# Masking the blocks of an attention state: four scaled ScalarE copies in the place of one VectorE product

## The chip, the cores and the metric

The kernel runs on one core of a Trainium2 chip. The time is the device time of one execution in microseconds. TensorE does the matrix products, VectorE (DVE), ScalarE (ACT) and GpSimd (POOL) the elementwise work, and SyncE (SP) issues the transfers. Each engine works through its own queue in the order in which the program was written; semaphores tie the queues together.

## The reference

Three parts follow one another. The first is a chunked linear attention with decay over 4 batches, 8 heads, 768 positions, head width 32 and state width 16:

```
for c in chunks:
    cum = cumsum(log(clip(a)))                       # per head, within the chunk
    M = (C B^T) * exp(cum_i - cum_j) * causal
    y = M x + (C state) * exp(cum_i)
    state = exp(cum_last) * state + sum_j B_j x_j exp(cum_last - cum_j)
```

The heads are then put side by side (256 features, 3072 tokens). The second part is `h = max(x w1, x w2, x w3)` with 768 hidden features and `h w_out`. The third is `h = x w_in` with 2048 hidden features, a rational function of h (cubic polynomial over quadratic), and a product with a second `w_out`. The weights come as 64-bit floating-point numbers, the result is float32.

## The kernel before, in words

The attention works in 6 chunks (NG) of 128 positions (CH). In each chunk there are 8 units (NU): a batch and a half of the heads. A head occupies a part of the 128 partitions, four heads interleaved: partition p belongs to head p mod 4 of its half. For each unit TensorE makes the decay's exponents in PSUM (`d_mm`, lines 482 to 504; ScalarE takes the exponential, line 504), the products of C and B (`s_mm`, line 477), VectorE multiplies the two (`m_op`, line 509), and TensorE makes the output of the chunk (`y_intra`, line 520). The influence of earlier chunks is added from the state (`y_inter`, line 531).

After each chunk but the last, `state(g)` (lines 549 to 580) renews the state. Sixteen products of B with x go into one PSUM buffer of 128 x 512 (line 555), four column blocks of 128, one for each batch. They hold all pairs of four heads; only the pairs of a head with itself are wanted. So the columns are in four groups of 32, one for each head, and on partition p only group p mod 4 may stay. The 0/1 table `own` (128 x 128, loaded with the coefficients into `co_raw`, line 332) says which. The function `mask` (lines 565 to 568) multiplies with it. For the first chunk the masked product is the state itself, in SBUF. For the other four it is masked in place in PSUM, and four VectorE instructions (`upd`, lines 570 to 575) add it to the decayed state before. The PSUM buffer comes from the ring `pd` of two, which the decay exponents of `d_mm` and a product for `e0` (line 455) use too: a decay product two places later waits until the updates have read the buffer.

The weights are converted on the way in, 28 pieces of 256 rows x 256 columns (`plan_conv`, lines 213 to 263): a transfer into one of three raw buffers, two ScalarE steps (lines 246 and 249), three VectorE steps (lines 247, 250 and 253; the last frees the raw buffer), two GpSimd additions (line 258), a ScalarE copy into the high part (line 196) and two GpSimd subtractions for the low part (line 262). 20 pieces belong to the phase of the attention and may run beside it or after it; the last 8 are the second `w_out`.

The order of all this is not written by hand. `Plan` (lines 51 to 153) takes each operation with its engine, an estimated cost, what it reads and writes, and for the matrix products a due time. It works out the latest time of each operation from its followers, then runs a list schedule with the estimated costs: the engine that is free first takes, of the operations that are ready by then, the one with the earliest latest time. The order that results is what each engine's queue gets. The operations of the two later parts (phase 1) are let in when all of the attention (phase 0) is placed. All transfers go through SP's queue, in the planned order, each waiting for its buffer.

The two later parts run column block after column block of 512 tokens, with every float32 product as three products of high and low parts (`mm3`, lines 646 to 652).

Of the kernel before, what the change touches and what calls it, by code (L numbers as in the profile page):

```python
# [13 lines left out]
AF = mybir.ActivationFunctionType  # L14
ALU = mybir.AluOpType
# [3 lines left out]
NB, NH, SEQ, HD, NS = 4, 8, 768, 32, 16  # L19
CH = 128  # L20
# [30 lines left out]
class Plan:  # L51
# [16 lines left out]
    def op(self, engine, cost, fn, reads=(), writes=(), at=None, behind=()):  # L68
        i = len(self.ops)
        deps, after = set(), {w for t in behind for w in t.writers}  # L70
        for t in reads:
            assert (t.writers or t.given) and not t.closed
            deps.update(t.writers)
            t.readers.append(i)
        for t in writes:
            assert not t.closed
            if t.first is None:
                t.first = i
                if t.before and not t.before.given:
                    after.add(t.before.first)  # L80
                if t.prev:
                    t.prev.closed = True
                    deps.update(t.prev.writers + t.prev.readers)
            deps.update(t.writers + t.readers)
            t.writers.append(i)
        deps.discard(i)
        after.discard(i)
        self.ops.append((engine, cost, fn, [t for t in writes if t.first == i], deps, after, at,
                         self.phase))
# [67 lines left out]
def decay_attention_max_moe_rational_moe(  # L157
# [19 lines left out]
    act, dve, pool, pe = nc.scalar, nc.vector, nc.gpsimd, nc.tensor  # L177
# [93 lines left out]
    op = plan.op  # L271
    pools = {"mp1": mp1}

    def new(pl, tag, size, shape=(128, T), dtype=F32):
        return plan.tile(tag, size, lambda: pools[pl].tile(list(shape), dtype, tag=tag, name=tag))
# [56 lines left out]
    own = co_raw[:, 6:]  # L332
# [76 lines left out]
    for p in range(3):  # L409
        src = pcv if p == 0 else (lambda p=p: cr(p - 1))  # L410
        op("act", 0.3, lambda p=p, src=src: copy(act, cs[:, p], src()), [pc if p == 0 else cr_t], [cs_t])
        if p < 2:
            op("dve", 0.34, lambda p=p, src=src: dve.tensor_tensor(out=cr(p), in0=src(), in1=cs[:, p],
                                                                   op=ALU.subtract),
# [9 lines left out]
    def load_cum(g):  # L424
# [12 lines left out]
        out=sel.rearrange("r (q n f) -> r q n f", q=2, f=4),  # L437
        in_=ld[1][0:24, :, 0].rearrange("r (q f) -> r q f", q=2)[:, :, None, :].to_broadcast([24, 2, NS, 4])),
# [5 lines left out]
    def book(key, cost):  # L444
        when[key] = clock[0]
        clock[0] += cost
# [102 lines left out]
    def state(g):  # L549
        t = new("pd", "d", 2)  # L550

        def mm():
            for b in range(NB):
                for q in range(2):
                    pe.matmul(t.t[64 * q:64 * q + 64, 128 * b:128 * b + 128],
                              bg[g].t[:, 2 * b + q].rearrange("j n f -> j (n f)"),
                              xg[g].t[:, b, 128 * q:128 * q + 128],
                              start=(b == 0), stop=True, skip_group_check=True,
                              tile_position=(0, 64 * q))
        book(("st", g), 0.6)  # L560
        op("pe", 0.6, mm, [bg[g], xg[g]], [t], when["st", g])
        st[g + 1] = o = new("s2", "st", 2)


        def mask(out):
            dve.tensor_tensor(out=out.rearrange("p (b x) -> p b x", b=NB),
                              in0=t.t.rearrange("p (b x) -> p b x", b=NB),
                              in1=own[:, None, :].to_broadcast([128, NB, CH]), op=ALU.mult)

        def upd():  # L570
            for b in range(NB):
                c = slice(128 * b, 128 * b + 128)
                dve.scalar_tensor_tensor(
                    out=o.t[:, c], in0=st[g].t[:, c], scalar=e0[g].t[:, 128 * b + 127:128 * b + 128],
                    in1=t.t[:, c], op0=ALU.mult, op1=ALU.add)
        if g == 0:
            op("dve", 0.68, lambda: mask(o.t), [t, own_t], [o])
        else:
            op("dve", 0.68, lambda: mask(t.t), [own_t], [t])
            op("dve", 1.2, upd, [t, e0[g], st[g]], [o])  # L580

    plan.phase = None
# [15 lines left out]
    for s in range(NS_ALL + LEAD + 3):  # L598
        if s < NS_ALL:
            d_mm(s)  # L600
            if s % NU == NU - 1 and s // NU + 2 < NG:
                load_cum(s // NU + 2)
        u = s - LEAD
        if 0 <= u < NS_ALL:
            g, k = divmod(u, NU)
            if u % 2 == 0:
                s_mm(u)
            m_op(u)
            if k == NU - 1 and g + 2 < NG:
                load_s(g + 2)  # L610
            if k == 4 and g + 1 < NG:
                prep(g + 1)
        u = s - LEAD - 1
        if 0 <= u < NS_ALL:
            g, k = divmod(u, NU)
            y_intra(u)
            if k == 2 and g < NG - 1:
                state(g)
            if k == 3 and g:
                y_inter(g)  # L620
            if k >= NU - 2:
                y_out(g, k - NU + 2)
            if k == NU - 1 and g + 2 < NG:
                load_v(g + 2)
# [343 lines left out]
```

## Time and profile before

| | us |
|---|---|
| median of 3 runs | 578.93 (577.61 to 580.32) |
| profiled execution | 579.21 |
| its span | 577.3 |
| TensorE busy | 556.8 (96%) |
| VectorE busy | 511.9 (89%) |
| ScalarE busy | 435.3 (75%) |
| GpSimd busy | 440.6 (76%) |

The span runs from the first to the last instruction of the profiled execution. Busy times are sums over the span; an engine can be idle for long in one stage and full in another. The mean granted clock of TensorE is 0.997 of full speed.

### The profile page before, as it was taken

The page shows a single profiled execution, that of the slowest core. Times are in us where ns is not written, and L with a number is a line of the kernel's source. Part 1 is how long each engine was busy: PE and PEld are TensorE (multiplying, and loading weights), DVE is VectorE, ACT ScalarE, POOL GpSimd, SP SyncE. Part 2 cuts the span into 40 slices and gives each one's busy share as a digit, 9 for nine tenths or more (in the row PEclk, how much of TensorE's full clock was granted, in tenths as well). Part 3 has the DMA queues.
Part 4 walks back from the last instruction along what each step waited for, and adds up shares of the span by engine and source line. Part 5 has one row for each costly group of instructions (what it writes and reads, how often), then busy time and mean ns, then how long its engine had stood idle before and what let it go on. Part 6 is the DMA issues. An engine that isn't in the chain of part 4 may idle for free.

```text
span 577.3 us, 8164 instructions
## 1 busy us (share of the span) xinstructions
PE 556.8 (96%) x2747; PEld 411.2 (71%) x2758; DVE 511.9 (89%) x777; ACT 435.3 (75%) x756; POOL 440.6 (76%) x410
## 2 busy tenths in 40 slices
PE   8989989989999999999999999999999999999997
PEld 3333433768787788888888888888888888886563
DVE  7888979777999999998889988898898889988996
ACT  4677768556888878878788787778777877778883
POOL 1756767887989967778677877687777997869883
PEclk9999999999999999999999999999999999999999
DMA  6877864533000000101000010000000010000000
GB/s 216 243 270 238 237 233 148 182 110 109 1 1 2 18 20 0 37 1 38 0 1 37 1 33 6 0 20 18 1 1 1 0 37 0 1 1 36 2 0 36
DMA packets 19047, 33.71 MB, mean 58 GB/s; under 512 B 3526, under 2 KB 4030, under 8 KB 19006
## 3 DMA queue, kind: packets, MB, share of 16 engines
q1 hardware_dynamic: 19003, 33.20, 17.9%
q8 instruction: 21, 0.34, 0.2%
q14 instruction: 23, 0.16, 0.1%
HBM read 27.27 MB, written 5.91 MB: 57 GB/s over the span
## 4 chain that ended last, share of the span: by engine, by line
PE 53%; DVE 17%; POOL 17%; issue 4%; ACT 4%; DMA 3%; SPq 2%; POOLq 0%; ACTq 0%; DVEq 0%
PE pg L650 7%; PE pg L652 7%; PE pg L651 6%; PE ph L650 5%; PE ph L652 5%; PE ph L651 5%; PE po L652 4%; PE po L650 4%; PE po L651 4%; POOL glo L853 2%; PE s L477 2%; DMA wraw<-in_w_dram 2%; POOL v L819 2%; POOL hlo L295 2%; DVE pr L845 2%
## 5 line engine op out<-in xcount | busy, mean ns | idle before, releaser
L853 POOL TENSOR_TENSOR glo<-w,ghi 128x512 fp32r<-128x512 f32 x80 | 105.5, 1319 | 16.2 <-ACT ghi L196 16.1
L650 PE MATMUL pg<-xhi,w_hi 128*128 128x512 f32 x202 | 79.1, 392 | 2.8 <-DVE xa L732 2.2
L652 PE MATMUL pg<-xhi,w_lo 128*128 128x512 f32 x202 | 78.8, 390 | 0.0
L651 PE MATMUL pg<-xlo,w_hi 128*128 128x512 f32 x202 | 78.7, 390 | 0.0
L840 ACT ACTIVATE pr<-v,qc 128x512 f32<-128x512 f32 x83 | 57.4, 693 | 22.2 <-DVE v L826 11.3
L295 POOL TENSOR_TENSOR hlo<-xa,hhi 128x512 fp32r<-128x512 f32 x36 | 49.5, 1376 | 26.0 <-ACT hhi L196 25.9
L258 POOL TENSOR_TENSOR wa<-wa,we 128x256 uint32<-128x256 uint32 x56 | 44.2, 800 | 32.9 <-DVE wa L253 32.9
L196 ACT ACTIVATE ghi<-w 128x512 fp32r<-128x512 f32 x80 | 50.4, 630 | 23.9 <-PE po L652 14.2
L650 PE MATMUL ph<-yhi,win_hi 128*128 128x512 f32 x160 | 62.7, 392 | 1.7 <-DVE w L838 1.5
L651 PE MATMUL po<-glo,wo_hi 128*128 128x512 f32 x160 | 62.4, 390 | 0.4 <-POOL glo L853 0.4
L652 PE MATMUL ph<-yhi,win_lo 128*128 128x512 f32 x160 | 62.3, 390 | 0.0
L650 PE MATMUL po<-ghi,wo_hi 128*128 128x512 f32 x160 | 62.3, 390 | 0.0
L652 PE MATMUL po<-ghi,wo_lo 128*128 128x512 f32 x160 | 62.3, 390 | 0.0
L651 PE MATMUL ph<-ylo,win_hi 128*128 128x512 f32 x160 | 62.3, 389 | 0.0
L845 DVE SCALAR_TENSOR_TENSOR pr<-w,co,pr 128x512 f32<-128x512 f32 x83 | 61.9, 746 | 0.0
L819 POOL TENSOR_TENSOR v<-t,v 128x512 f32<-128x512 f32 x44 | 58.1, 1320 | 2.8
L842 DVE SCALAR_TENSOR_TENSOR v<-v,pr 128x512 f32<-128x512 f32 x83 | 56.2, 677 | 2.2 <-ACT pr L841 2.2
L847 DVE SCALAR_TENSOR_TENSOR w<-v,pr 128x512 f32<-128x512 f32 x83 | 56.3, 678 | 0.4
L841 ACT ACTIVATE pr<-pr 128x512 f32<-128x512 f32 x86 | 50.5, 587 | 0.9
L732 DVE TENSOR_TENSOR xa<-xa,pg 128x512 f32<-128x512 f32 x67 | 45.5, 679 | 2.3 <-PE pg L652 2.1
L650 PEld LDWEIGHTS pg<-xhi,w_hi 128*128 128x128 f32 x202 | 37.9, 188 | 12.1 <-DVE xa L732 3.1
L837 POOL TENSOR_TENSOR w<-w,t 128x512 f32<-128x512 f32 x20 | 25.9, 1293 | 24.0 <-DVE v L826 22.1
(167 smaller groups left out, 1485.1 us busy)
## 6 DMA issues: line engine op xcount, KB each, us to landing
wraw<-in_wo_dram SPq DMA_DIRECT2D x11, 512.0 KB
wraw<-in_w_dram SPq DMA_DIRECT2D x9, 512.0 KB
wraw<-in_win_dram SPq DMA_DIRECT2D x8, 512.0 KB
xn<-in_xn_dram SPq DMA_DIRECT2D x6, 512.0 KB
out_dram<-ob SPq DMA_DIRECT2D x12, 256.0 KB
xt_d<-xo SPq DMA_DIRECT2D x10, 256.0 KB
xst<-xt_d SPq DMA_DIRECT2D x10, 256.0 KB
bt<-in_bz_dram SPq DMA_DIRECT2D x6, 256.0 KB
```

The costliest lines, as they stand in the source:

```text
L196: act.activation(out=o, in_=i, func=AF.Copy)
L295: lambda: e.tensor_tensor(out=lo.t, in0=src(), in1=hi.t.bitcast(F32), op=ALU.subtract),
L650: pe.matmul(dst, wh, hi, start=first, stop=False)
L651: pe.matmul(dst, wh, lo, start=False, stop=False)
L652: pe.matmul(dst, wl, hi, start=False, stop=last)
L819: pop(1.23, lambda: pool.tensor_tensor(out=f(v), in0=f(t1), in1=f(v), op=ALU.mult), [t1], [v])
L840: aop(0.62, lambda: act.activation(out=f(r), in_=f(v), func=AF.Ln, bias=qc), [v], [r])
L841: aop(0.48, lambda: act.activation(out=f(r), in_=f(r), func=AF.Exp, scale=-1.0), [], [r])
L842: dop(0.61, lambda: dve.scalar_tensor_tensor(out=f(v), in0=f(v), scalar=QC, in1=f(r), op0=ALU.add, op1=ALU.mult), [r], [v])
L845: dop(0.61, lambda: dve.scalar_tensor_tensor(out=f(r), in0=f(w), scalar=c(0), in1=f(r), op0=ALU.add, op1=ALU.mult), [w], [r])
L847: dop(0.61, lambda: dve.scalar_tensor_tensor(out=f(w), in0=f(v), scalar=2.0, in1=f(r), op0=ALU.subtract, op1=ALU.mult), [v, r], [w])
L853: pop(1.23, lambda: pool.tensor_tensor(out=f(lo), in0=f(w), in1=f(hi).bitcast(F32), op=ALU.subtract), [w, hi], [lo])
```

## The change

The mask goes from VectorE to ScalarE. Column group f of every batch block (4 blocks x 32 columns) is copied with a scale that is read per partition: the column 32 f of `own`, which is 1 on the partitions of head f and 0 on the others. Four such copies make the mask. The planner is told that the operation is ScalarE's and costs 1.2 us, where it was VectorE's and 0.68. What is read and written is unchanged, in place for four of the five states.

```
         def mask(out):
-            dve.tensor_tensor(out=out.rearrange("p (b x) -> p b x", b=NB),
-                              in0=t.t.rearrange("p (b x) -> p b x", b=NB),
-                              in1=own[:, None, :].to_broadcast([128, NB, CH]), op=ALU.mult)
+            for f in range(4):
+                act.activation(out=out.rearrange("p (b f d) -> p f b d", b=NB, f=4)[:, f],
+                               in_=t.t.rearrange("p (b f d) -> p f b d", b=NB, f=4)[:, f],
+                               func=AF.Copy, scale=own[:, HD * f:HD * f + 1])
...
         if g == 0:
-            op("dve", 0.68, lambda: mask(o.t), [t, own_t], [o])
+            op("act", 1.2, lambda: mask(o.t), [t, own_t], [o])
         else:
-            op("dve", 0.68, lambda: mask(t.t), [own_t], [t])
+            op("act", 1.2, lambda: mask(t.t), [own_t], [t])
             op("dve", 1.2, upd, [t, e0[g], st[g]], [o])
```

## Rows read from the trace of the kernel before

**Rows 1.** Stretches: us, busy (x instructions) by engine, granted clock, DMA share, GB/s.
```profile
0.00:30.00 30.00, 26.67 (x149) 10.75 (x151) 23.58 (x41) 17.39 (x31) 13.52 (x19) 1.00 0.79 229
30.00:60.00 30.00, 27.31 (x255) 11.82 (x260) 27.45 (x50) 23.20 (x43) 20.08 (x23) 1.00 0.77 256
60.00:100.00 40.00, 34.67 (x341) 14.69 (x345) 35.54 (x61) 30.03 (x54) 28.36 (x37) 1.00 0.65 206
100.00:130.00 30.00, 27.20 (x117) 21.26 (x118) 22.65 (x29) 17.33 (x31) 25.39 (x29) 0.95 0.42 143
130.00:190.00 60.00, 58.32 (x254) 47.22 (x253) 54.45 (x79) 47.44 (x84) 53.90 (x52) 1.00 0.08 27
190.00:500.00 310.00, 310.00 (x1369) 256.75 (x1368) 280.80 (x413) 241.59 (x411) 240.91 (x198) 1.00 0.04 13
```

**Rows 2.** Groups of the mask's line on VectorE: busy us, mean ns, idle before.
```profile
L566 DVE TENSOR_TENSOR d<-d,co_raw 128x512 f32<-128x512 f32 x4 | 2.8, 689 | 0.4 <-PE d L555 0.4
...
L566 DVE TENSOR_TENSOR st<-d,co_raw 128x512 f32<-128x512 f32 x1 | 0.7, 692 | 0.0
```

**Rows 3.** ScalarE groups with each shape apart, whole span.
```profile
L825 ACT ACTIVATE v<-ph,co 128x512 f32<-128x512 f32 x40 | 27.1, 677 | 0.0
...
L816 ACT ACTIVATE v<-ph 128x512 f32<-128x512 f32 x40 | 23.8, 595 | 2.7 <-PE ph L652 2.1
...
L840 ACT ACTIVATE ph<-v,qc 128x256 f32<-128x256 f32 x1 | 0.5, 479 | 0.5 <-POOL v L810 0.5
...
L841 ACT ACTIVATE ph<-ph 128x256 f32<-128x256 f32 x1 | 0.4, 368 | 0.0
...
L440 ACT ACTIVATE co<-co_raw 128x2 f32<-128x2 f32 x1 | 0.2, 193 | 0.0
```

**Rows 4.** Timeline by engine, 48 to 55 us: start, us, instruction, idle before and releaser.
```profile
49.17 1.09 PE L555 MATMUL d<-xn,bn 128*64 128x128 f32 x16
...
52.77 0.39 PE L488 MATMUL d<-trib 128*128 128x512 bf16 x1 [0.83 <-DVE st L573]
...
50.32 0.70 DVE L566 TENSOR_TENSOR d<-d,co_raw 128x512 f32<-128x512 f32 x1 [0.36 <-PE d L555]
50.93 0.75 DVE L250 TENSOR_SCALAR wa<-wa 128x512 uint32<-128x512 uint32 x1
51.60 1.11 DVE L573 SCALAR_TENSOR_TENSOR st<-st,e,d 128x128 f32<-128x128 f32 x4
...
49.80 0.66 ACT L249 ACTIVATE we<-wraw 128x512 uint32<-128x512 uint32 x1
50.37 0.58 ACT L504 ACTIVATE e<-d 128x512 f32<-128x512 f32 x1
51.43 0.68 ACT L246 ACTIVATE wa<-wraw 128x512 f32<-128x512 f32 x1 [0.48 <-POOL w_lo L262]
```

**Rows 5.** Timeline by engine, 79 to 88 us.
```profile
82.27 1.09 PE L555 MATMUL d<-xn,bn 128*64 128x128 f32 x16
...
84.94 0.37 PE L455 MATMUL d<-re,sel 24*128 24x512 bf16 x1 [0.68 <-ACT e L504]
85.69 0.38 PE L488 MATMUL d<-trib 128*128 128x512 bf16 x1 [0.38 <-DVE st L573]
...
83.58 0.69 DVE L566 TENSOR_TENSOR d<-d,co_raw 128x512 f32<-128x512 f32 x1
...
84.52 1.11 DVE L573 SCALAR_TENSOR_TENSOR st<-st,e,d 128x128 f32<-128x128 f32 x4
...
84.29 0.60 ACT L504 ACTIVATE e<-d 128x512 f32<-128x512 f32 x1 [1.05 <-PE d L490]
```

**Rows 6.** Waits of TensorE, 0 to 100 us: total us, times, longest.
```profile
PE d L488 <- DVE st L573: 1.2, 2, 0.8
```

**Rows 7.** Waits of SP's queue, 0 to 100 us.
```profile
SPq L241 <- DVE wa L253: 17.3, 6, 6.3
SPq L283 <- PE y L531: 2.3, 2, 1.3
```

## The prediction

> **What bounds the kernel now.** I read first the busy time by stretch [rows 1], then the group of the line that goes [rows 2], the ScalarE groups that give the price of what comes [rows 3], and the instructions around the single states [rows 4, 5], last the waits [rows 6, 7].
>
> The stretches show three regimes. From 190 to 500 us TensorE is busy 310.0 of 310.0: nothing that happens in the attention stage reaches that part except by moving it as a whole. From 0 to 100 us the attention runs with the conversion of the weights between its instructions: TensorE is busy 26.67 + 27.31 + 34.67 = 88.65 us, VectorE 23.58 + 27.45 + 35.54 = 86.57, ScalarE 17.39 + 23.20 + 30.03 = 70.62. From 100 to 190 the first products run beside the last conversions; TensorE lacks 2.80 us of 30 and 1.68 of 60 there, and its granted clock is 0.95 in the first of the two stretches [rows 1]. So all that an edit of the attention can gain or lose is TensorE's idle time before 190 us, 11.35 + 4.48 = 15.8 us, plus what the lower clock costs; much of the 11.35 is start-up, before any state exists. VectorE has 13.4 us of slack in the first 100 us and ScalarE 29.4. That alone speaks for moving work from VectorE to ScalarE, but a stage with every engine at 70 to 90% and a written order on each is bound by whichever result comes last, now of one engine, now of another. The question is which states' masks lie on such a chain.
>
> **The change part by part.** *Removed:* five VectorE products, four in PSUM of 689 ns and one into SBUF of 692 ns [rows 2], 4 x 0.689 + 0.692 = 3.45 us of VectorE. In the queue each takes a little less than it lasts, since the next starts before its end.
>
> *Added:* twenty ScalarE copies, each 128 partitions x 128 elements in runs of 32, with a per-partition scale. The trace has no such instruction, so I take it from its neighbours [rows 3]. From PSUM without a per-partition operand 512 elements take 595 ns, with one (a scale) 677: 82 ns for the operand. Without one, 256 elements take 368 ns and 2 elements 193: (368 - 193) / 254 = 0.69 ns an element, while 256 to 479 ns with one is 111 ns more. So 128 elements: 193 + 0.69 x 126 + 82 = 362 ns, at most 391 with the 111. Neighbours in the queue overlap: the 0.66 us instruction at 49.80 is followed at 50.37, 0.09 us before its end [rows 4]. Four in a row: 3 x (0.37 - 0.09) + 0.37 = 1.21 us. Bounds: 4 x 0.193 = 0.77 us if the length cost nothing and nothing overlapped, and 4 x 0.479 = 1.92 us if the runs of 32 made each as dear as the 256-element one with its operand. I take 1.21, nearest to the row of the same operand count, so five masks are 6.0 us of ScalarE (3.9 to 9.6). None hides on its own; what hides it is ScalarE's 29.4 us of slack.
>
> The Trainium skill (ScalarE: Activation LUTs, What ACT_TABLE_LOAD costs) gives 186 ns + 0.833 ns an element, about 93 more for a per-partition operand, and 93 of overlap. By it a copy would be an estimated 386 ns and four 1.27 us, and the forecast would not move. The same page (Rules for kernel authors) would keep multiplications on VectorE. In instruction time the trace agrees, 0.69 us against 1.21; what the rule leaves out is how full either engine is, and that it speaks against this change is the second rival below.
>
> *Moved, state by state.* A state's path is: state products on TensorE, mask, four updates on VectorE, then the two-buffer PSUM ring is free for the next decay product and the state for the inter-chunk products. All waits of the decay product on the update sum to 1.2 us in 2 cases, 0.8 the longer [rows 6]. So of five masks only two are felt; the other three have slack, and their longer mask (1.21 - 0.69 = 0.52 us and a hand-over between engines) costs nothing there.
>
> The first felt state [rows 4]: the state products end at 49.17 + 1.09 = 50.26. The product starts at 50.32 and ends at 51.02, but VectorE then does a conversion step until the updates start at 51.60. With ScalarE, which finishes a conversion instruction at 50.46 and has an exponential next, the mask could run from 50.37 to 51.58, and with a hand-over like the 0.06 us between TensorE and VectorE just seen, up to some 0.2, the updates start at 51.64 to 51.78: 0.04 to 0.18 us later. TensorE waited 0.83 us there, so this goes straight into the end. If the exponential at 50.37 goes first, add its 0.58. The other way, the conversion step that stood between can go ahead of the updates at no cost; a gain there is excluded by the mask's end. I take +0.1 (bounds 0 to +0.8).
>
> The second [rows 5]: the state products end at 83.36, the mask ran 83.58 to 84.27, the updates from 84.52, and TensorE waited 0.38 for them at 85.69. ScalarE was idle until 84.29. The mask on it runs 83.42 to 84.63, the updates start at 84.7 to 84.8: +0.2 to +0.3. The exponential of 84.29 moves to 84.54 or later; the product at 84.94 had waited 0.68 for it, so it moves by 0.25 too, alongside, not on top. I take +0.25 (bounds 0 to +1.2, if the mask goes behind that exponential and a conversion).
>
> *The relief of VectorE:* behind each mask the queue moves up by 0.69 us at most. What is late next? The weight transfers stand in SP's queue until the last conversion step on VectorE frees a raw buffer: 17.3 us of such waits in 6 cases before 100 us [rows 7]. Each earlier release brings a transfer, its ScalarE steps and GpSimd's work forward. But ScalarE's own steps of the same conversion go back by the 1.21 us of a mask. At the first felt state a conversion step stood right behind the mask, at 50.93 [rows 4], and such a step could come 0.69 us earlier; as the two effects meet in one conversion I count half of that once, -0.35 (bounds 0 and -3.45, all five masks).
>
> Sum: +0.1 + 0.25 - 0.35 = 0.0 us. The profiled execution took 579.21 us, its span 577.3 and 1.9 around it; that is 0.28 above the median of the runs, 578.93, and inside their spread of 577.61 to 580.32. Forecast: 579.2 us, no change.
>
> **Rivals.** *First, VectorE is the true bound of 30 to 100 us.* For it: it is busy 27.45 of 30 and 35.54 of 40, and holds the raw buffers [rows 1, 7]. Then all 3.45 us come off: 579.2 - 3.45 = 575.8. Against it: TensorE is busy 27.31 of the same 30, so most of what VectorE gives up is met by TensorE's own queue, and what is gained in the conversions counts only as far as it fills the 4.48 us that TensorE lacks between 100 and 190 us.
>
> *Second, slower: ScalarE's queue is held at the mask.* Its place is the head of ScalarE's queue when the four copies wait for the state products. VectorE waited 0.36 us in that position at 50.32 [rows 4]; behind the copies on ScalarE stand exponentials, for which TensorE already waits (0.68 at 84.94 [rows 5]), and the conversion's absolute value, low word and high part, for which VectorE and GpSimd wait. Price: 0.36 + 1.21 = 1.57 us of ScalarE for each state. It decides once ScalarE has less idle time near a state than that. Around the states at 50 and 84 it had 0.48 and 1.05 us [rows 4, 5], so the point is near. With three crowded states of five, 3 x 1.57 = 4.7 us less what VectorE's relief returns, 0.35: 583.6. Nor does it end there: the inter-chunk products are later with the state, and the loads behind them in SP's in-order queue (2.3 us in 2 cases already [rows 7]) and the weights behind those. Against it: 29.4 us of slack over the stage, and the planner knows of the copies, as it is given 1.2 us for them.
>
> *Third, the order is drawn anew.* The planner sees other costs and engines, so all queues of the attention and its conversions may come out differently, not only around the masks. Then the stall of TensorE between 100 and 130 us, 2.80 us and about 0.05 x 30 = 1.5 us by the clock [rows 1], may vanish or double: 574.9 or 583.5. For it: the stage has 48 decay products and 28 conversions that can slide past one another. Against it: their due times are those of before.
>
> *Fourth, the copies cost what the dear bound says,* 1.92 us: (1.92 - 1.21) x 2 felt states = +1.4 us, 580.6; this stays within no change.
>
> **How the numbers follow.** Forecast with the fourth 0.50; VectorE the bound 0.18; ScalarE held 0.23; the new order 0.09, of it 0.05 to the slow side. About 0.5% is what a measurement of this kernel can tell from no change, 2.9 us either way of 578.93. Faster: 0.18 + 0.04 = 0.22. Slower: 0.23 + 0.05 = 0.28. Same: 0.50. The forecast's own range is 576.9 to 581.4: below it the lowest of the runs, 577.61, less twice the 0.35; above it 579.2 with the 0.8 of the first felt state and the 1.4 of the dear copies. To leave out no more than 2 in 10 the range reaches to the first rival on one side and past the second on the other: 575.3 to 584.2.
>
> **What would show it.** Right: in the profile after, twenty copies of about 0.36 us, four in about 1.2; VectorE 3.4 us less and ScalarE about 6 more by the sum of the busy time; the wait of the decay product on the updates still 1 to 2 us in all; TensorE still full from about 190 us. The first rival shows as fewer waits of SP's queue on the conversion step, and a TensorE that is full earlier. The second shows as ScalarE waiting for the state products by name, and more waits of TensorE on exponentials. The third shows as another order of conversions, and another idle time between 100 and 130 us. The prediction is wrong if TensorE's idle time before 190 us changes by over 3 us in either direction.

## The result, and the profile after

Over 22 executions each, the kernel after takes 582.52 us (579.47 to 585.43) and the kernel before 578.92 (576.93 to 582.95): a ratio of 1.0051, interval 1.0036 to 1.0066. That lies inside the stated range and at the 0.5% from which the prediction called a kernel slower: the interval reaches to both sides of it. The most likely case, no change at 579.2 us, was 3.3 us off. An execution over 1.5% longer than the fastest of its kernel (there is one, of the copies told 0.68 us below) is left out of its time and ratio.

The profiled execution after took 582.59 us, its span 580.8. Its stretches, in the columns of [rows 1]:

```profile
0.00:30.00 30.00, 26.50 (x151) 10.88 (x152) 23.57 (x40) 18.41 (x36) 13.21 (x19) 1.00 0.80 238
30.00:60.00 30.00, 26.41 (x228) 11.37 (x227) 24.57 (x45) 22.07 (x44) 16.73 (x21) 0.89 0.69 226
60.00:100.00 40.00, 35.29 (x315) 14.58 (x314) 33.99 (x55) 32.51 (x63) 30.10 (x39) 1.00 0.68 222
100.00:130.00 30.00, 27.49 (x169) 20.44 (x168) 23.30 (x35) 18.93 (x33) 24.94 (x28) 1.00 0.40 142
130.00:190.00 60.00, 57.98 (x249) 46.27 (x250) 53.25 (x76) 47.25 (x83) 52.97 (x52) 1.00 0.08 27
190.00:500.00 310.00, 310.00 (x1369) 256.78 (x1368) 280.72 (x414) 241.68 (x410) 240.12 (x197) 1.00 0.04 13
```

From 190 to 500 us TensorE is as full as before, so all was decided earlier. The change shows between 30 and 60 us: 228 matmuls were done there, 255 before [rows 1], at a granted clock of 0.89. Some matmul records are missing in the trace of before; by the weight loads, the counts of the next column, of which none is missing, it is 227 and 260. The groups of the mask and of the update, with each shape apart:

```profile
L567 ACT ACTIVATE d<-d,co_raw 128x128 f32<-128x128 f32 x16 | 5.4, 340 | 2.0 <-PE d L555 1.5
...
L574 DVE SCALAR_TENSOR_TENSOR st<-st,e,d 128x128 f32<-128x128 f32 x16 | 4.5, 342 | 4.3 <-ACT d L567 4.3
...
L567 ACT ACTIVATE st<-d,co_raw 128x128 f32<-128x128 f32 x4 | 1.1, 368 | 0.4 <-PE d L555 0.4
```

VectorE now waits 4.3 us for the copies. TensorE's waits of 0 to 100 us, the answer to [rows 6]:

```profile
PE d L488 <- ACT e L504: 1.9, 3, 1.2
PE y L520 <- ACT e L504: 1.4, 1, 1.4
...
PE s L477 <- DVE m L509: 0.9, 1, 0.9
PE y L520 <- ACT xo L196: 0.9, 1, 0.9
...
PE d L455 <- DVE st L574: 0.4, 1, 0.4
```

The wait on the updates, 1.2 us before, is down to 0.4: the state's own path is not where TensorE waits. It waits for exponentials, products and output copies that are placed otherwise. Three instructions of the timeline show the low clock and the state whose products begin at 37.85 us. The first, the four records of a pair of C and B products, spans 3.00 us here and 1.13 at 41 us; not all of that is the clock, as the same pair takes 2.06 at a clock of 1.00 in the profile of the experiment below that fills TensorE's idle time:

```profile
31.97 3.00 PE L477 MATMUL s<-cz,bt 64*128 64x512 f32 x4 [0.92 <-DVE m L509]
...
39.65 1.47 ACT L567 ACTIVATE d<-d,co_raw 128x128 f32<-128x128 f32 x4 [1.53 <-PE d L555]
...
41.15 1.12 DVE L574 SCALAR_TENSOR_TENSOR st<-st,e,d 128x128 f32<-128x128 f32 x4 [3.79 <-ACT d L567]
```

Read alone, this profile has a ready story. TensorE's idle time is the same (577.3 - 556.77 = 20.5 us before, 580.8 - 559.79 = 21.0 after), and its busy time is 3.0 us longer, because matmuls from 32 to 39 us ran at the lower of its two clock levels, 1.2 GHz. A part of it falls with the count of the records of line 490, the second matmul of a decay product, first before, then after:

```profile
L490 PE MATMUL d<-lr x29: 376/379/380, 24.1 to 94.8; 128*128 128x512 bf16 x29
```

```profile
L490 PE MATMUL d<-lr x40: 377/379/634, 24.6 to 103.9; 128*128 128x512 bf16 x40
```

Eleven are missing before, and the gaps that they leave (0.05 to 0.15 us each) sum to 1.3 us that are counted as idle. So TensorE is an estimated 1.7 us longer busy and 1.8 us longer idle. The profiles of the copies in the old order, the product in the new order, the copies to SBUF and the idle time filled lack the same kind of record, 11 each, and can be compared with one another. The experiments show that what is left of the story belongs to this one execution.

### The profile page after: what moved, and what is told of

The parts are those of the page before. It is cut to its first block, busy times and chain, and to the rows that moved or that the text cites. A ratio compares the mean times of both kernels' runs of the same rounds, so it can differ in the third digit from the quotient of the medians.

```text
span 580.8 us, 8190 instructions
## 1 busy us (share of the span) xinstructions
PE 559.8 (96%) x2758; PEld 411.9 (71%) x2758; DVE 509.5 (88%) x772; ACT 442.4 (76%) x776; POOL 439.5 (76%) x410
## 4 chain that ended last, share of the span: by engine, by line
PE 50%; POOL 20%; DVE 17%; issue 5%; ACT 5%; DMA 2%; SPq 0%; POOLq 0%; DVEq 0%; ACTq 0%
PE pg L651 6%; PE pg L652 6%; PE pg L653 6%; PE ph L651 4%; PE ph L652 4%; PE ph L653 4%; PE po L651 4%; PE po L652 4%; PE po L653 4%; POOL glo L854 3%; POOL wa L258 3%; POOL hlo L295 2%; POOL v L820 2%; DVE wa L253 2%; POOL wo_lo L262 2%
```

## The experiments

Three theories. A: the new order of all queues costs, whatever makes the mask. B: the copies cost, by their length and by what stands behind them on ScalarE. C: the clock costs. The second set split A: any new order is a draw (A1), a plan with the mask on ScalarE is worse as such (A2), the plan was given too low a cost (A3). Each set of kernels was timed against the kernel before in five rounds on one chip; there were three sets, so compare ratios, not times, between sets.

**The copies in the order of before.** In the kernel after, only what the planner is told goes back:

```
-            op("act", 1.2, lambda: mask(t.t), [own_t], [t])
+            op("dve", 0.68, lambda: mask(t.t), [own_t], [t])
```

and so for the first state. Apart from the mask, all five queues then hold the instructions of before in their order; the two traces agree on that instruction by instruction.

> The four ScalarE copies, but the planner is still told that the mask is VectorE's and costs 0.68 us, so all queues keep the order of before and the copies stand in ScalarE's queue where the program reaches them. If the new order is what costs (theory A), the time is that of before, 579 plus or minus 1 us. If the copies themselves on ScalarE cost (theory B: 1.45 us in place where the product took 0.69, and what stands behind them), it is that of the change, about 582.5.

Measured: 580.08 us, ratio 1.0016 (1.0002 to 1.0029): 0.1 us above the upper end of what theory A expected, 2.4 below theory B.

**The product in the order of the change.** The opposite edit in the kernel before: the VectorE product, told as `"act", 1.2`.

> The VectorE product, but the planner is told that the mask is ScalarE's and costs 1.2 us, so all queues have the order of the change. Theory A (the order): about 582.5 us, with TensorE idle from 28.7 to 32 us and its granted clock low in 30 to 40 us, as after the change. Theory B (the copies): 579 plus or minus 1.

Measured: 582.29 us, ratio 1.0060 (1.0036 to 1.0083). So the order alone gives the whole of the 0.51%, and without it the copies cost 0.16%, 0.9 us. Theory A stands and, of B, those 0.9 us are left. The stretch of 30 to 60 us in the two profiles, first the copies in the old order:

```profile
30.00:60.00 30.00, 27.61 (x255) 11.96 (x259) 26.15 (x48) 25.34 (x50) 20.37 (x23) 1.00 0.78 256
```

and the product in the new order:

```profile
30.00:60.00 30.00, 25.50 (x223) 11.04 (x226) 24.72 (x45) 20.84 (x38) 17.05 (x23) 0.89 0.69 220
```

255 matmuls and 223, as in the kernels before and after, 255 and 228 (by weight loads 259 and 226, 260 and 227); the count follows the order, not the engine of the mask.

The executions of that set also bear on C. Their mean granted clock over the span was 0.9953 for the kernel before (26 executions) and 0.9952 for the product in the new order (10). Among those with 0.997 or more, the medians are 578.6 us (10 executions) and 581.6 (5). The difference of 3.0 us is there at an equal clock. The clock moves both kernels: before from 576.65 us at 1.000 to 582.15 at 0.991, the product in the new order from 579.87 at 1.000 to 583.95 at 0.991.

**TensorE's idle time filled.** In the kernel after:

```
-            for q, t in enumerate(ts):
+            for q, t in [z for z in enumerate(ts) for _ in range(2 if u == 10 else 1)]:
...
-            op("pe", 0.46, lambda: mm(lambda: ld[g % 2][:, k], lambda: rd[g % 2]),
+            op("pe", 0.46, lambda: [mm(lambda: ld[g % 2][:, k], lambda: rd[g % 2]) for _ in range(3 if u == 12 else 1)],
```

> The change, but TensorE repeats two products of which the results stay the same: the sixth pair of C and B products once more (1.06 us) and the thirteenth decay product twice more (0.9 us), just before and in its idle time of 28.7 to 32 us. If the drop of the granted clock after that idle time is what costs (theory C), the clock stays at its upper level from 30 to 40 us and the time falls by about 3 us, to 579.5, though work was added. If the order costs by its waits alone, the time stays at 582.5 or rises by up to 1.

Measured: 581.59 us, ratio 1.0038 (1.0020 to 1.0056). Its stretch:

```profile
30.00:60.00 30.00, 25.58 (x234) 11.24 (x238) 25.93 (x46) 23.64 (x48) 17.78 (x23) 1.00 0.71 228
```

The clock is 1.00 now, and still only 234 matmuls are done, four of them repeats, and the kernel is 0.38% slower than before. Of the 3 us that C promised 0.8 came by the ratios (1.0051 to 1.0038), and the intervals of this kernel and the one after overlap. The mean clock of its nine executions is 0.998, that of the kernel after 0.996. In this profile and in that of the copies in the old order the clock is 1.00 throughout the attention, so TensorE's idle time can be compared: 30 - 25.58 = 4.42 us here from 30 to 60 us, 30 - 27.61 = 2.39 there. The other stretches up to 190 us differ by 0.2 together (14.56 and 14.32). In these two profiles, what the new order costs in idle time lies between 30 and 60 us.

**The copies to SBUF.** In the kernel after, in the order of the change:

```
+    ms = [sp.tile([128, T], F32, name=f"ms{i}") for i in range(2)]
...
-                    in1=t.t[:, c], op0=ALU.mult, op1=ALU.add)
+                    in1=ms[g % 2][:, c], op0=ALU.mult, op1=ALU.add)
...
-            op("act", 1.2, lambda: mask(t.t), [own_t], [t])
+            op("act", 1.2, lambda: mask(ms[g % 2]), [own_t], [t])
```

> The change, but the four later states are copied from PSUM into an SBUF buffer instead of in place; the planner is told the same, so the order is that of the change. If masking in place makes each copy wait for the one before, four copies take 1.14 us as for the first state, not 1.46. Theory B then expects up to 4 x 0.3 = 1.3 us less, 581.2; theory A no difference beyond 0.5 us, 582.5.

Measured: 582.65 us, ratio 1.0060 (1.0038 to 1.0083), no gain. The copies did get shorter in a row: on ScalarE the mask of the third state is

```profile
53.23 1.14 ACT L568 ACTIVATE ms<-d,co_raw 128x128 f32<-128x128 f32 x4
```

against 1.46 in place. In place the program makes each copy wait on ScalarE's own semaphore for the one before it, and they start 0.36 to 0.37 us apart; to SBUF it does not, and they start 0.25 to 0.27 apart. But the updates, which now read two operands from SBUF, took twice as long:

```profile
L575 DVE SCALAR_TENSOR_TENSOR st<-st,e,ms 128x128 f32<-128x128 f32 x16 | 10.0, 686 | 1.0 <-ACT ms L568 1.0
```

**More buffers for the output copies.** In the kernel after, `xo = new("s4", "xo", 2)` for `new("s2", "xo", 2)`: four real buffers, two in the plan.

> The change, with four SBUF buffers in place of two for the copied-out outputs xo; the planner still counts two, so the order is that of the change to the last instruction. In that order the output copy of the second chunk waits 1.0 us on ScalarE for a VectorE subtraction that was placed late, and TensorE 0.9 to 1.3 us behind it at 48 to 50 us. If that wait is a part of what the order costs, the two waits vanish and the time falls by 0.5 to 1.3 us, to 581.2 to 582.0; if TensorE meets the next wait instead (the exponential before the state products, 0.7 us), under 0.3 us.

Measured: 583.72 us, ratio 1.0066 (1.0040 to 1.0092): nothing gained. The 0.9 us wait for the output copy is gone between 38 and 64 us; all of TensorE's waits that this stretch has are

```profile
PE y L520 <- DVE m L509: 1.9, 1, 1.9
PE d L455 <- DVE st L574: 0.6, 1, 0.6
PE d L488 <- ACT e L504: 0.4, 1, 0.4
```

The next wait took its place. The one wait that was tried does not carry the 3 us.

**Other orders.** Nothing but the cost that the planner is told of the mask is changed, in the kernel after (1.5, 0.9, 0.68 for 1.2) and in the kernel before (0.6, 0.8, 1.0 for 0.68).

> The change, but the planner is told 1.5 us for the four copies, near the 1.46 that they take in place; the order is drawn anew by that. Theory A1 (any new order is a draw, the time of a drawn order scatters by some us whoever makes the mask): anywhere from 578 to 585. Theory A2 (a plan with the mask on ScalarE is worse as such): 582 to 584. Theory A3 (the plan was worse since its cost was too low): 579 to 580.

> The change, but the planner is told 0.9 us for the four copies. A1: anywhere from 578 to 585, with no line through 0.9, 1.2 and 1.5. A2: 582 to 584. A3: 583 to 585, worse than with 1.2, since the cost is further off.

> The kernel before, with the VectorE product, but the planner is told 0.60 us for it (what it holds VectorE's queue for) in place of 0.68. Nothing that runs is changed but the order. A1: anywhere from 577 to 584, away from 579.5 by 1 us or more with even chances. A2: 579.5 plus or minus 1.

> The change, but the planner is told that the ScalarE copies cost 0.68 us, what it was told of the product. A1 (each order is a draw): anywhere from 580 to 586. A2 (a plan with the mask on ScalarE is worse as such): 582 to 584, as with 0.9 and 1.2.

> The kernel before, but the planner is told 0.8 us for the product. The order is nearer to that of before than any other drawn here. If a few places decide (A1 with a local cause), within 1 us of 579; if any redrawing costs since the order of before is a lucky one, 581 to 584, as with 0.6.

> The kernel before, but the planner is told 1.0 us for the product; an order further from that of before. A1: anywhere from 579 to 585, and not better for being nearer to what the planner was told of the copies. A2 (only ScalarE's plan is worse): 579 plus or minus 1.

Measured, with the change itself:

| mask by | cost told, us | time, us | ratio to before |
|---|---|---|---|
| VectorE | 0.60 | 582.64 | 1.0069 (1.0043 to 1.0095) |
| VectorE | 0.68 | before | 1 |
| VectorE | 0.80 | 580.89 | 1.0027 (1.0007 to 1.0046) |
| VectorE | 1.00 | 582.65 | 1.0048 (1.0026 to 1.0070) |
| ScalarE | 0.68 | 583.64 | 1.0072 (1.0048 to 1.0097) |
| ScalarE | 0.90 | 583.09 | 1.0074 (1.0047 to 1.0101) |
| ScalarE | 1.20 | 582.52 | 1.0051 (1.0036 to 1.0066) |
| ScalarE | 1.50 | 593.01 | 1.0234 (1.0210 to 1.0258) |

With the product unchanged, a told cost that is 0.08 us lower makes the kernel 0.69% slower, more than the change did: A1 is shown. A3 falls, as 1.5 is nearest to the measured 1.46 and far the worst. A2 as it was expected, with VectorE's plans within 1 us of before, falls too, by 0.60 and 1.00. That ScalarE's plans are worse on the average isn't settled: they are 0.51 to 0.74% and 2.34% slower, those with VectorE 0.27 to 0.69%, and the intervals overlap. The order nearest to that of before, 0.80, came out at 580.89 us, between the two times that were expected of it, and decides nothing. All seven new orders are slower than that of before; why that one is the best of eight stays open.

A new order can cost by the clock too. The executions told 0.60, 0.80 and 1.00 have mean clocks of 0.9923, 0.9946 and 0.9928, those of before in their sets 0.9961 and 0.9957. The two told 1.00 with 0.997 took 578.60 and 579.78 us, while 13 of before with 0.997 have a median of 579.40: for that order no loss is seen at an equal clock. The copies told 0.90 lost 0.74% at 0.9963, as high as before. With 1.5 the stretch of 30 to 60 us is

```profile
30.00:60.00 30.00, 25.21 (x189) 9.68 (x190) 22.73 (x36) 20.21 (x40) 17.43 (x21) 0.77 0.65 217
```

and there the clock matters most: all four executions had a mean of 0.981 to 0.986. In its profile TensorE is busy 565.42 us and its span is 591.1. Of 13.8 us more than before, 8.65 are busy time and 5.2 idle; with the 1.3 us of records that are missing before, an estimated 7.4 and 6.4.

**The product to SBUF.** In the kernel before, in its own order, the four later masks go to SBUF and the updates read them there, with the two edits of the copies to SBUF.

> The kernel before in its own order, but the four later products go from PSUM into an SBUF buffer, from which the updates read, so that the PSUM buffer comes free 1.1 us earlier. TensorE waited 1.2 us for it in 2 cases: if that is worth its length, 578.0 to 578.5, better than both kernels. But with the copies to SBUF the updates took 0.81 us instead of 0.34 at the median; if it is the SBUF operand that does this and not the order, VectorE loses up to 16 x 0.47 = 7.5 us and the time is 580 to 583.

Measured: 579.55 us, ratio 1.0004 (0.9990 to 1.0019), the same. The updates:

```profile
L574 DVE SCALAR_TENSOR_TENSOR st<-st,e,ms 128x128 f32<-128x128 f32 x16 | 6.2, 444 | 0.0
```

at 444 ns instead of the 335 to 342 with the mask in PSUM. The earlier release of the PSUM buffer bought nothing measurable. TensorE's wait on the updates is gone from 0 to 100 us, but the decay product waits 2.1 us for exponentials, where it waited 1.3 before. No version that was tried beats the kernel before.

## Why the prediction was right or wrong

**The range and the sum.** The range held the time, in part by luck: no change was forecast, and the range reached to 584.2 for the second rival, whose cause was not the one. The sum of 0.0 us was worked out instruction by instruction in the order of before, and for that order it was off by the 0.9 us of the copies in the old order. What failed is the step beneath it: the sum carried the old order over to the changed kernel. The instructions around the states at 50 and 84 us [rows 4, 5], on which it rests, have other neighbours after the change.

**The sign of being wrong.** TensorE's idle time before 190 us went from 15.83 to 16.33 us, an estimated 1.8 us more with the missing records, so the sign set at 3 us did not show. It looked at one execution of each kernel, and at idle time alone.

**The copy's price.** Forecast 0.36 us each and 1.21 for four; measured 0.368 and 1.14 for the first state, which goes to SBUF. In place one is 0.340, but four take 1.46, since each waits for the one before. The overlap of 0.09 us in the sum was the term at fault, 1.46 against 1.21, inside the bounds of 0.77 to 1.92. ScalarE got 5.4 + 1.1 = 6.5 us of copies where 6.0 were forecast, and its busy time rose by 442.4 - 435.3 = 7.1; VectorE's fell by 2.4, not 3.4.

**The felt states.** Forecast +0.1 and +0.25 at two states, and the wait on the updates at 1 to 2 us in all. In the profile after, it is 0.4; it is 0.3 with the copies in the old order and 1.3 with the product in the new order. VectorE's queue takes the wait: 4.3 us after, 3.8 of it at one state, while TensorE had other products to do.

**VectorE's relief.** Counted at -0.35. No run shows it by itself. The copies in the old order, with VectorE relieved and ScalarE loaded, were no faster; the first rival, which had 3.45 us come off, is refuted by that.

**The second rival,** ScalarE held at the mask, named the right sign and nearly the time (583.6), but the wrong cause: with the copies and all that stands behind them in the old order, 0.9 us is what was left of 4.7. ScalarE did wait for the state products, 1.5 us once, as that rival said; it cost little. TensorE's waits on the exponentials of line 504 from 0 to 100 us rose from 3.2 us to 4.0, but to 4.6 with the product in the new order: they too go with the order.

**The third rival,** the order drawn anew, is what happened. It had a chance of 0.09 and 0.05 on the slow side. The time it gave, 583.5, was near; its place, TensorE's stall of 100 to 130 us, was not: idle time there is 2.51 us after and 2.80 before [rows 1], and the loss sits between 30 and 60 us. Its argument against, that the due times were those of before, carried no weight: in the attention due times are given to matmuls alone, and all else follows from the told costs. A told cost that changes on an operation between engines should have had most of the chance for a change, with a width of some us, in place of the 0.50 for none; all seven draws here fell on the slow side.

What stays open: why an order with fewer matmuls done from 30 to 60 us isn't caught up, and which of its places decides. One wait was removed without effect, and the idle time refilled with little.

## What to carry to other kernels

Where a planner writes the order, a small edit is two changes: what it does, and a new draw of every queue behind it. Separate them before explaining either, once with the new instructions in the old order and once with the old instructions in the new order; and draw a few more orders with nothing else changed, to see how far a time moves for no reason of the edit. A stretch at a low clock in one profile is a reading of one execution; compare kernels at equal clocks before making it the cause, and look at the mean clock of all executions, as an order can also be one that runs at a lower clock.

## What the runs showed of the hardware

After similar idleness (1.81 us before and 2.12 after, from 28 to 32 us) the clock fell in one profile and held in the other. In the columns of [rows 1], first the kernel before, where the clock held:

```profile
28.00:32.00 4.00, 2.19 (x12) 0.67 (x8) 1.29 (x3) 3.02 (x6) 0.65 (x1) 1.00 1.00 290
32.00:36.00 4.00, 3.42 (x31) 1.59 (x34) 4.00 (x8) 3.08 (x7) 2.25 (x3) 1.00 0.44 160
```

then the kernel after, where it went to the lower level:

```profile
28.00:32.00 4.00, 1.88 (x9) 0.41 (x5) 1.71 (x4) 3.17 (x6) 0.81 (x2) 0.96 0.90 283
32.00:36.00 4.00, 4.00 (x10) 1.22 (x14) 4.00 (x9) 0.62 (x2) 1.77 (x2) 0.50 0.50 156
```

The second surprise is the update that reads its mask from SBUF. With the copies to SBUF four of them last 2.59 us at a place where GpSimd works without a pause from 56.15 us on. First VectorE's timeline, then GpSimd's:

```profile
55.89 2.59 DVE L575 SCALAR_TENSOR_TENSOR st<-st,e,ms 128x128 f32<-128x128 f32 x4
```

```profile
56.15 0.73 POOL L258 TENSOR_TENSOR wa<-wa,we 128x256 uint32<-128x256 uint32 x1 [1.18 <-DVE wa L253]
56.83 0.77 POOL L262 TENSOR_TENSOR w_lo<-wa,w_hi 128x256 fp32r<-128x256 f32 x1
57.57 0.77 POOL L258 TENSOR_TENSOR wa<-wa,we 128x256 uint32<-128x256 uint32 x1
58.30 0.78 POOL L262 TENSOR_TENSOR w_lo<-wa,w_hi 128x256 fp32r<-128x256 f32 x1
```

The four updates end at 58.48 us, soon after the fourth GpSimd instruction begins. The Trainium skill (SBUF — State Buffer, "SBUF: two separate sides") states that a VectorE operation with two SBUF inputs and a GpSimd operation that reads SBUF take turns by whole instructions. The 686 ns against 342 agree with it; that the wait is this one was not tried by itself.
